# Taking the transposes of q, k and x from the matrix engine to DMA, in a sliding-window attention followed by a dense layer pair

## The chip, the cores and the metric

One core of one Trainium2 chip. The metric is the device time of one execution in microseconds (us). All comparisons are between fast runs. PE is TensorE, ACT ScalarE, DVE VectorE, POOL GpSimd, SP SyncE; on SP nothing but DMA is issued here.

## The reference, cut to what matters

```python
# q, k, v: (8 batches, 8 heads, 576, 64) f32, drawn with 0.1 standard deviation
scores = (1 / sqrt(64)) * q @ k^T
mask   = (0 <= i - j < 64)                 # window of 64, causal
attn   = softmax(where(mask, scores, -1e9))
x      = (attn @ v) as (4608 tokens, 512)  # heads side by side
h      = x @ w_in                          # 512 -> 2048
out    = (h - tanh(h)) @ w_out             # 2048 -> 512
```

## The kernel before

The kernel interleaves two streams of work on PE by hand. One is the pair of dense layers, cut into 9 chunks of 512 tokens with 16 tiles of the hidden layer each; a *half step* is four wide matmuls of the first layer or of the second. The other is the attention, cut into 32 *groups* (a batch and a pair of heads, four groups a batch). `at(h, f)` places a piece of attention behind half step `h`; in the steady part one group takes eight half steps. The first three batches are placed by a script (`PLAN`), batches 3 to 7 by a loop. The matmuls take q, k and x transposed; the kernel transposes them on PE, by matmuls against an identity.

```python
def load_all(b, n):                        # a whole batch of q or k, f32 -> bf16 on the way
    t = all_pool.tile([P, H, E * D], BF16, tag=n, name=n + "all")
    nc.gpsimd.dma_start(out=t, in_=(q if n == "q" else k)[b].rearrange(...))
    # ... (cut)

def keys_v(b, j, eng=nc.sync):             # V's rows into the place of the keys, DMA inside SBUF
    eng.dma_start(out=vw[b % 2][64:128, j]..., in_=vb[8 * j:8 * j + 8]...)

def shift_v(b, j0, j1, eng=nc.sync):       # the same rows once more, shifted by one block of 64
    # ... (cut) one DMA from vw[b % 2][64:128] to vw[b % 2][0:64]

def tr(g, which, bank, *engs):             # six transposes of 96x128 on PE, then copies out of PSUM
    # ... (cut)
    for e in range(E):
        nc.tensor.transpose(tp[:, e, :], src[:, e, :], ident[:P, :P])
    # ... (cut) q: the two heads' halves into separate columns, zeros between; k: as it is

def scores(g, grp, bank):                  # three matmuls of 128 rows x 128 columns, both heads at once
    # ... (cut)
    nc.tensor.matmul(sp[:, i, :], kT[g % NR][:, 64 * j:64 * j + 128],
                     qT[g % NR][:, :, 64 * j:64 * j + 64], ...)
    nc.scalar.activation(PT[...], sp, ACT.Exp, scale=scale)

def y_out(c, s):                           # the second layer's result: copied by ACT, stored by SP
    nc.scalar.activation(ysb, ps[:, yp_bank(c, s), :], ACT.Copy)
    nc.sync.dma_start(out=out[r0:r0 + 128, :], in_=ysb)

for g in range(3 * NP, B * NP):            # batches 3 to 7
    b, pr = divmod(g, NP)
    a = 8 * g - 48
    # ... (cut: casts)
    at(a, tr, g, "q", 3, nc.scalar, nc.vector)
    at(a + 2, tr, g, "k", 3, nc.scalar)
    for i in range(3):
        at(a + 5 + 2 * i, scores, g, i, 4)
    # ... (cut: masking, pv, norm)
    if pr % 2 == 1:
        at(a + 20, x_tr, b, pr // 2, 0, 4, 3)
        at(a + 22, x_tr, b, pr // 2, 4, NJ, 3)
    # ... (cut: keys_v nine times from 32 * b - 54)
    if pr == 0:
        at(32 * b - 78, load_v_all, b)
        at(32 * b - 64, load_all, b, "q")
        at(32 * b - 63, load_all, b, "k")
        at(32 * b - 47, shift_v, b, 0, NJ - 1)
```

The softmax here doesn't subtract the row's maximum and nothing guards it: scores larger than these inputs give would overflow.

## Time and profile before

| kernel before | value | where it is from |
|---|---|---|
| device time, median of 3 | 361.99 us | the runs |
| span of the profiled run | 362.1 us | the page's head |
| PE busy | 326.2 us, 90% | busy by engine |
| PE's mean granted clock | 0.995 | list of cores |
| DMA engines in 120 to 160 us | 0.62 of their time | busy by stretch, last column but one |
| what the chain that ended last consists of | PE 73%, DMA 15% | chain |

The strips, stretches and timelines that this rests on stand in the prediction below. Of the waits of PE, the largest is the first row; each row is "who waits, for whom: us in total, times, longest". The page's row of the hardware DMA queue (packets, megabytes, and the time these packets took as a share of the span of all 16 engines).

```profile
PE ps L197 <- DVE qb L81: 7.7, 2, 6.2
PE ps L224 <- DMA vw<-vw: 0.2, 1, 0.2
```

```profile
q1 hardware_dynamic: 10904, 17.69, 17.0%
```

### The profile page before, as it was taken

How to read it: one execution, taken by the hardware profiler on the slowest of the kernel's cores; microseconds unless marked ns; L12 is line 12 of the kernel's file. 1: busy time of each engine (PE TensorE's matmuls, PEld its weight loads, DVE VectorE, ACT ScalarE, POOL GpSimd, SP SyncE). 2: the span in 40 equal slices, each digit the busy share in tenths (PEclk: the TensorE clock that was granted, in tenths of full speed). 3: DMA queues.
4: the chain of work that ended last, by engine and by line, in shares of the span. 5: the costliest groups of instructions: out<-in, count | busy, mean ns of one | idle time of the engine just before them, and what ended most of it. 6: DMA issues, size and time to landing. Idle time of an engine off the chain costs nothing.

```text
span 362.1 us, 6043 instructions
## 1 busy us (share of the span) xinstructions
PE 326.2 (90%) x2329; PEld 189.5 (52%) x2329; DVE 214.7 (59%) x352; ACT 192.8 (53%) x355; POOL 103.6 (29%) x136
## 2 busy tenths in 40 slices
PE   0538667889999999999999999999999999999995
PEld 0438345655555555555555555555555544444442
DVE  3418657775676776767677767677676633443300
ACT  2536364876656656565656555655564444443421
POOL 7809522806319309312830272110000000000000
PEclk9999998999999999999999999999999999999999
DMA  8899992377876567655935592250000010010012
GB/s 158 128 218 200 216 222 54 54 137 114 202 155 92 97 163 123 129 99 121 139 84 108 128 129 74 58 127 31 30 32 29 31 58 29 31 57 29 31 67 78
DMA packets 31948, 36.76 MB, mean 102 GB/s; under 512 B 3472, under 2 KB 25872, under 8 KB 31536
## 3 DMA queue, kind: packets, MB, share of 16 engines
q0 software_dynamic: 20384, 17.90, 32.7%
q1 hardware_dynamic: 10904, 17.69, 17.0%
q10 hardware_dynamic: 632, 0.79, 0.7%
q8 instruction: 18, 0.29, 0.4%
q14 instruction: 10, 0.08, 0.1%
HBM read 36.70 MB, written 9.44 MB: 127 GB/s over the span
## 4 chain that ended last, share of the span: by engine, by line
PE 73%; DMA 15%; issue 5%; POOL 3%; ACT 2%; DVE 2%; SPq 0%; POOLq 0%; ACTq 0%; DVEq 0%
PE ps L278 32%; PE ps L259 29%; DMA vw<-vb 7%; DMA kall<-in_k_dram 4%; PE ps L224 4%; PE ps L197 3%; PE ps L210 3%; DMA vall<-in_v_dram 2%; PE ps L241 2%; DMA vw<-vw 1%; POOL kb L81 1%; POOL vb L81 1%; DVE qt L81 1%; ACT th L262 1%; POOL qb L81 0%
## 5 line engine op out<-in xcount | busy, mean ns | idle before, releaser
L259 PE MATMUL ps<-xT,wi 128*128 128x512 bf16 x576 | 148.2, 381 | 1.0 <-DVE gT L268 0.9
L278 PE MATMUL ps<-w_out_sb,gT 128*128 128x512 bf16 x576 | 145.2, 379 | 0.2 <-ACT ysb L283 0.2
L268 DVE TENSOR_TENSOR gT<-ps,th 128x512 bf16<-128x512 f32 x144 | 98.9, 690 | 74.2 <-ACT th L262 73.0
L262 ACT ACTIVATE th<-ps 128x512 f32<-128x512 f32 x144 | 86.0, 598 | 85.4 <-PE ps L259 84.1
L259 PEld LDWEIGHTS <-wi 128*128 128x128 bf16 x576 | 61.3, 114 | 47.0 <-issue 2.7
L278 PEld LDWEIGHTS <-gT 128*128 128x128 bf16 x576 | 53.6, 98 | 51.3 <-issue 0.5
L214 ACT ACTIVATE pt<-ps 128x384 bf16<-128x384 f32 x96 | 46.9, 491 | 48.5 <-PE ps L210 37.7
L81 POOL COPY vb<-vall 72x1024 bf16<-72x1024 bf16 x28 | 29.4, 1060 | 71.3 <-DMA vw<-vb 53.9
L235 DVE TENSOR_TENSOR xs<-ps,rc 64x576 bf16<-64x576 f32 x64 | 48.3, 755 | 1.5
L210 PE MATMUL ps<-qt,kt 128*128 128x128 bf16 x288 | 37.3, 230 | 5.6 <-ACT pt L214 3.1
L224 PE MATMUL ps<-vw,pt 128*128 128x130 bf16 x288 | 30.6, 229 | 8.5 <-DVE vw L133 7.1
L224 PEld LDWEIGHTS <-pt 128*128 128x128 bf16 x288 | 22.7, 102 | 22.5 <-issue 7.6
L81 POOL COPY qb<-qall 96x768 bf16<-96x768 bf16 x27 | 22.9, 848 | 36.2 <-PE ps L197 22.9
L81 DVE COPY qt<-ps 64x576 bf16<-64x576 bf16 x33 | 25.0, 757 | 12.9 <-ACT qt L79 8.3
L81 POOL COPY kb<-kall 96x768 bf16<-96x768 bf16 x28 | 23.6, 847 | 28.9 <-DMA kall<-in_k_dram 11.1
L210 PEld LDWEIGHTS <-kt 128*128 128x128 bf16 x288 | 25.0, 104 | 10.8 <-ACT kt L79 2.4
L283 ACT ACTIVATE ysb<-ps 128x512 f32<-128x512 f32 x36 | 21.4, 594 | 15.1 <-PE ps L278 15.1
L81 DVE COPY xT<-ps 128x512 bf16<-128x512 bf16 (+4 forms) x35 | 12.1, 368 | 16.8 <-PE ps L241 16.8
L197 PE MATMUL ps<-ident,qb 96*128 96x96 bf16 x192 | 14.4, 215 | 7.9 <-DVE qb L81 7.7
L79 ACT ACTIVATE qt<-ps 64x576 bf16<-64x576 bf16 x31 | 19.7, 635 | 3.5 <-PE ps L197 1.9
L79 ACT ACTIVATE kt<-ps 128x576 bf16<-128x576 bf16 x30 | 19.4, 645 | 2.6 <-PE ps L197 1.5
L197 PE MATMUL ps<-ident,kb 96*128 96x96 bf16 x192 | 14.4, 214 | 5.7 <-ACT kb L79 4.6
(47 smaller groups left out, 148.0 us busy)
## 6 DMA issues: line engine op xcount, KB each, us to landing
out_dram<-ysb SPq DMA_DIRECT2D x36, 256.0 KB
vw<-vb SPq DMA_DIRECT2D x67, 65.0 KB
vall<-in_v_dram POOLq DMA_DIRECT2D x7, 576.0 KB, 9.2
kall<-in_k_dram POOLq DMA_DIRECT2D x7, 576.0 KB, 10.2
qall<-in_q_dram POOLq DMA_DIRECT2D x7, 576.0 KB, 6.3
vw<-vw SPq DMA_DIRECT2D x6, 520.0 KB
w_out_sb<-in_moe_w_out_dram POOLq DMA_DIRECT2D x4, 512.0 KB, 13.3
wi<-in_moe_w_in_dram POOLq DMA_DIRECT2D x2, 512.0 KB, 14.0
```

What stands on the lines that cost most here:

```text
L79: nc.scalar.activation(o, i, ACT.Copy)
L81: eng.tensor_copy(o, i)
L197: nc.tensor.transpose(tp[:, e, :], src[:, e, :], ident[:P, :P])
L210: nc.tensor.matmul(sp[:, i, :], kT[g % NR][:, 64 * j:64 * j + 128], qT[g % NR][:, :, 64 * j:64 * j + 64], start=True, stop=g >= 2 * NP)
L214: nc.scalar.activation(PT[g % NPT][:, 3 * grp:3 * grp + 3, :], sp, ACT.Exp, scale=scale)
L224: nc.tensor.matmul(ps[:, 5 + grp, 130 * i:130 * i + 130], PT[g % NPT][:, j, :], vw[b % 2][:, j, 2 * pr:2 * pr + 2, :], start=True, stop=True)
L235: nc.vector.tensor_tensor(xo[r, :, :, pr, :], ov[r, :, :, h, 0:D], rc[r].to_broadcast([64, 3, 3, 64]), ALU.mult)
L259: nc.tensor.matmul(hp, w_in_tile(ki, m), chunk_tile(c)[:, ki, :], start=(ki == 0), stop=(ki == 3))
L262: nc.scalar.activation(th, hp, ACT.Tanh)
L268: nc.vector.tensor_tensor(gT[c][:, m, :], hp, th, ALU.subtract)
L278: nc.tensor.matmul(yp, gT[c][:, m, s * 128:(s + 1) * 128], w_out_sb[:, m, :], start=(m == 0), stop=(m == M - 1))
L283: nc.scalar.activation(ysb, ps[:, yp_bank(c, s), :], ACT.Copy)
```

## The change

The intent: take work off PE, the bound engine. In batches 3 to 7, q and k (already bf16) go through a scratch tensor in DRAM and come back transposed by DMA, two groups at a time; the output x of the attention is transposed by DMA straight into the dense layer's input. With q no longer padded with zeros, a score block is two matmuls of 64 rows, one for each head, on the upper and the lower half of the PE array ("row tiles"). The loads of q and k are issued ten half steps earlier, and the script of the first three batches was rewritten.

```diff
+    def bounce(n):                                  # SBUF -> DRAM
+        t = dram.tile([S, 256], BF16, tag=n, name=n + "d")
+        nc.sync.dma_start(out=t.rearrange("(p e) c -> p (e c)", e=E),
+                          in_=two[n].rearrange("p e i h d -> p (e i h d)"))
+        two[n] = t
+    def tr2(g, n):                                  # DRAM -> SBUF, transposed
+        o = qT2[g // 2 % 2] if n == "q" else kT2[g // 2 % 2][:, :, 64:]
+        nc.sync.dma_start(out=o, in_=two.pop(n), transpose=True)
+    def x_dma(b):                                   # two or three pieces, one for each chunk touched
+        ...
+            nc.sync.dma_start(out=chunk_tile(c)[...], in_=xs[b % 2][...], transpose=True)
+    def scores2(g, grp):
+        ...
+        for w in range(3):
+            j = 3 * grp + w
+            for h in range(2):
+                r = slice(64 * h, 64 * h + 64)
+                nc.tensor.matmul(sp[:, w, h, :], kT2[i][r, g % 2, 64 * j:64 * j + 128],
+                                 qT2[i][r, g % 2, 64 * j:64 * j + 64], start=True, stop=True)
 ... (cut: the new script of batches 0 to 2, buffers, the layout of xT)
     for g in range(3 * NP, B * NP):
-        a = 8 * g - 48
-        at(a, tr, g, "q", 3, nc.scalar, nc.vector)
-        at(a + 2, tr, g, "k", 3, nc.scalar)
+        a = 8 * g - 50
+        if pr % 2 == 0:
+            for i, n in enumerate("qk"):
+                at(a - 15 + 2 * i, cast2, g, n)
+                at(a - 14 + 2 * i, cast2, g + 1, n)
+                at(a - 12 + 2 * i, bounce, n)
+                at(a - 7 + 2 * i, tr2, g, n)
-            at(a + 5 + 2 * i, scores, g, i, 4)
+            at(a + 5 + 2 * i, scores2, g, i)
-        if pr % 2 == 1:
-            at(a + 20, x_tr, b, pr // 2, 0, 4, 3)
-            at(a + 22, x_tr, b, pr // 2, 4, NJ, 3)
+        if pr == NP - 1:
+            at(a + 18, x_dma, b)
-            at(32 * b - 64, load_all, b, "q")
-            at(32 * b - 63, load_all, b, "k")
+            at(32 * b - 74, load_all, b, "q")
+            at(32 * b - 73, load_all, b, "k")
```

## The prediction

Its sum came to -4.4 us, so 357.6, and the forecast to 358.5. Three terms are in part estimate:

- Mode switches (+8.4): the 0.07 us a switch was chosen between the extra of 0.107 us behind the mask's transpose, the one such place in the trace before, and half of that, since the clock had doubled by then. What PE does in that time is not shown.
- Row tiles (-2.0): that two of them can run at once was not shown before the change ran; the 28 ns a matmul and so the 5 us are worked out from the trace, the 0.4 is a guess. That weight loads lie hidden, which speaks for it, is read from the line for 120 to 160 us: PEld was busy for 23.35 of the 40 us (its second busy time) in which PE was busy for 40.00.
- Transfers (+1.5): from the 3.1 us for x's first piece and the two loads the author went on to about 8 us, the lead that x has, with a doubling for sharing and a latency that are not shown. "The trace has them" speaks of the DMA engines: their share is 0.62 and 0.57 in the lines for 120 to 200 us.

> **What bounds the kernel now.** I first read the busy shares in 40 slices, to see which stages there are, then the busy time by stretch.
>
> ```profile
> PE   0538667889999999999999999999999999999995
> ACT  2536364876656656565656555655564444443421
> DMA  8899992377876567655935592250000010010012
> ...
> 120.00:160.00 40.00, 40.00 (x301) 23.35 (x300) 27.93 (x48) 23.56 (x45) 15.99 (x19) 1.00 0.62 117
> 160.00:200.00 40.00, 40.00 (x304) 23.46 (x303) 28.98 (x47) 24.50 (x47) 12.72 (x15) 1.00 0.57 112
> 280.00:320.00 40.00, 40.00 (x198) 20.01 (x197) 17.70 (x29) 17.27 (x29) 0.00 (x0) 1.00 0.11 40
> ```
>
> There are three stages. Up to about 90 us PE has gaps and the DMA engines are full. From 90 to about 277 us the dense layers and the attention of the later batches share a full PE. After that the dense layers run alone. DVE (28 of 40 us) and ACT (24 of 40) bound neither later stage, so copies taken from them are worth nothing by themselves. The chain that ended last says the same: PE holds 73% of it.
>
> ```profile
> PE 73%; DMA 15%; issue 5%; POOL 3%; ACT 2%; DVE 2%; SPq 0%; POOLq 0%; ACTq 0%; DVEq 0%
> ```
>
> A busy PE is not a PE at its peak, so I read start times in the timeline of PE.
>
> ```profile
> 158.97 0.33 PE L210 MATMUL ps<-qt,kt 128*128 128x128 bf16 x3
> 159.14 1.03 PE L259 MATMUL ps<-xT,wi 128*128 128x512 bf16 x4
> 160.00 0.42 PE L197 MATMUL ps<-ident,qb 96*128 96x96 bf16 x6
> 160.37 1.02 PE L278 MATMUL ps<-w_out_sb,gT 128*128 128x512 bf16 x4
> 161.23 0.33 PE L210 MATMUL ps<-qt,kt 128*128 128x128 bf16 x3
> 161.40 1.03 PE L259 MATMUL ps<-xT,wi 128*128 128x512 bf16 x4
> 162.26 0.42 PE L197 MATMUL ps<-ident,kb 96*128 96x96 bf16 x6
> 162.52 0.38 PE L278 MATMUL ps<-w_out_sb,gT 128*128 128x512 bf16 x1
> ```
>
> From start to start four wide matmuls take 0.86 us (0.215 each), three score matmuls 0.17 us (0.056 each), and six k transposes 0.26 us (0.042 each). But the six q transposes take 0.37: 0.11 of it is a wait. The timeline of ACT at the same place names it.
>
> ```profile
> 159.34 0.49 ACT L214 ACTIVATE pt<-ps 128x384 bf16<-128x384 f32 x1 [0.72 <-PE ps L210]
> 159.73 0.59 ACT L283 ACTIVATE ysb<-ps 128x512 f32<-128x512 f32 x1
> ```
>
> The exp of the scores stands ahead of the output copy on ACT; the copy ends at 160.32, and only then may the second dense layer write its bank again (160.37). Once per eight half steps this happens. Where no q transpose stands in that place, the wait is seen whole:
>
> ```profile
> 273.68 1.03 PE L259 MATMUL ps<-xT,wi 128*128 128x512 bf16 x4
> 274.91 1.02 PE L278 MATMUL ps<-w_out_sb,gT 128*128 128x512 bf16 x4 [0.20 <-ACT ysb L283]
> ```
>
> 1.23 us from the start of the first layer's four matmuls to the second's, 0.86 of work and 0.37 of wait. So the q transposes lie wholly in the shadow of this wait, the k transposes do not.
>
> [...] The kernel before holds one instruction with 64 active rows, the transpose of the mask:
>
> ```profile
> 17.98 0.23 PE L183 MATMUL ps<-ident,seen 64*128 64x64 bf16 x1
> 18.14 0.42 PE L197 MATMUL ps<-ident,kb 96*128 96x96 bf16 x3
> ```
>
> 0.16 us pass to the next start. There the clock is still at half (128-column matmuls start 0.107 apart), so the 64 columns should take 0.053. About 0.107 is extra, with no wait recorded[...]. [...] No transpose by DMA is in the trace before, so no run shows it yet. [...] The trace has them 0.5 to 0.6 busy in the middle stage, so new traffic will queue with old.
>
> **The change part by part.** It touches 20 groups (head pairs) of 32, those of batches 3 to 7. The built program has 150 fewer matmuls.
>
> - Removed on PE: 12 transposes in each of 20 groups, 240 x 0.0417 = 10.0 us. Nine x transposes twice a batch for five batches, 90 x 0.057 = 5.1 us. Together 15.1 us.
> - The wait for the output copy stays, since score group 3 of the new schedule still stands just ahead of it, and nothing now fills it. It grows from 0.11 to 0.37 us less one switch of mode (0.07, below) that delays PE beside it: 0.30. Over 20 groups +3.8 us.
> - Scores: nine matmuls of 128 columns (9 x 0.056 = 0.50 us a group) become 18 of 64 columns. By the slope between 96 and 512 columns (0.418 ns a column and 1.5 ns) one takes 28 ns, so 18 take 0.51: no change if the two row tiles follow one another. If they run at once, 0.25 to 0.3 us a group is saved, 5 us in all. Each needs its own weight load of 128 columns, which may forbid it. I give it 0.4, so -2.0.
> - Mode switches: the scores of a group come in three places, each between 128-row matmuls, so six switches a group, 120 in all. Per switch I take [...]0.07. 120 x 0.07 = +8.4 us. This is the choice on which the sum hangs.
> - Copies: ACT loses 1.28 us and DVE 0.76 us a group plus the x copies. Off the path: 0. POOL makes as many copies as before.
> - Transfers: a pair of groups writes and rereads q and k through DRAM (each 295 KB), x moves 590 KB a batch. That is 5.9 + 5.9 + 2.95 = 14.7 MB more. The hardware queue's 17.69 MB took 17.0% of the span, 3.5 us a MB over 16 engines, so an estimate of 51 us of all engines over some 130 us: their share goes from about 0.55 to 0.9. The q and k transposes are issued 12 and 10 half steps (10 us or more) before use, which covers it. x is issued only eight half steps (about 8 us) before the first layer reads it, behind a q transpose and an output store on the same queue, while the next loads of q and k are issued. At 3.5 us a MB, x's first piece and those two (0.88 MB) take 3.1 us[...]. I expect little or no wait, at most 1 to 3 us at the first three chunks: +1.5.
> - Early stage: the script of the first three batches was rewritten. PE waited about 16 us between 40 and 120 us, so there is room, but also room to lose. Its loads of the first dense weights are issued later, those of the second batch's q earlier. I take -1 with 2.5 either way.
>
> Sum: -15.1 + 3.8 - 2.0 + 8.4 + 1.5 - 1.0 = -4.4, so about 357.6. Transfers can only add, so my median is 358.5.
>
> **The rivals.** (a) *The transposes come off PE almost freely*: switches cost 0.03 us or less, row tiles overlap. Then -15.1 + 4 - 5 + 3.6 - 1, about 348 us. For it: weight loads lie hidden everywhere in the trace before. Against it: the 0.16 us after the mask. (b) *Switches cost 0.12 us or more*: 14 us and no overlap give about +2, 364 us. For it: that 0.107 may be a fixed time, and entering the mode may cost more than leaving it. (c) *Transfers become the bound*: [...]x and then q and k come late, PE stands at each chunk, and 5 to 30 us are lost, 365 to 390. For it: the engines are already half busy and x has the smallest lead. Against it: the leads of q and k are ten half steps, and x's first piece shrinks from chunk to chunk. (d) *The early stage decides*: +-3 us whatever the middle does.
>
> **Range and chances.** Switches (+-3), overlap (-5 or 0) and the early stage (+-2.5) give about +-5 around 358; rival (c), at 0.15, stretches the upper side. Range 351 to 368. Faster by over 2% means under 354.8: it needs overlap or cheap switches, 0.30. Slower by over 2% means over 369.2: it needs (c) or dear switches with a bad early stage, 0.15 to 0.2. Within 2%: 0.5.
>
> **What would show each step.** In the timeline of PE of the changed kernel: score matmuls 28 ns apart (14 if tiles overlap); from the last matmul before a score group to the first of it, and on leaving, about 0.07 us more than the matmul's own time; 1.23 us from the first layer to the second at every eighth half step. Groups of 128x64 score matmuls: 360. PE's idle time by releaser should show no large entry from DMA to the first dense layer at 128 to 250 us; if it shows several us there, (c) was right. The first dense matmul should start near 40 us as now. I am wrong in the main if the middle stage's time per group changes by more than 0.4 us either way from 8.8 us (my sum: 8.8 - 0.76 + 0.19 - 0.1 + 0.42 = 8.55).

## The result, and the profile after

The changed kernel took 383.53 us (median of 4 fast runs, 382.12 to 384.88), the kernel before 361.86 us in the same rounds (4 runs, 361.65 to 362.25). The ratio is 1.060, with a 95% interval of 1.056 to 1.064: slower. Ratios in this document are the mean time of one kernel's fast runs over that of the other's of the same rounds, so not quite the ratio of the medians that are quoted. The prediction was 358.5 us with a range of 351 to 368; it was wrong.

First the strips of the changed kernel (40 slices of 9.5 us, busy tenths; PEclk is the granted clock), its stretches, and its chain by engine.

```profile
PE   1466879869849995989699979899999999999995
PEclk9999899998997998999899999999999999999999
DMA  8999995976994599779979897957700131001012
...
PE 52%; DMA 35%; ACT 4%; issue 3%; POOL 2%; DVE 1%; SPq 1%; POOLq 0%; DVEq 0%; ACTq 0%
```

```profile
120.00:160.00 40.00, 35.26 (x238) 17.64 (x241) 20.14 (x33) 17.99 (x34) 10.63 (x14) 0.96 0.75 149
160.00:200.00 40.00, 34.99 (x232) 17.26 (x235) 19.98 (x32) 17.00 (x33) 12.83 (x17) 0.96 0.90 175
280.00:320.00 40.00, 39.57 (x220) 19.80 (x224) 20.61 (x32) 18.14 (x32) 0.00 (x0) 1.00 0.16 48
```

PE, which was busy for 40.00 of 40 us in the two middle stretches, now has holes of five us in each, and its clock falls below full around them. The DMA share rose from 0.57 to 0.90 in the second one. In the chain PE gave up 21 points and DMA gained 20. (The third stretch now holds the last of the attention, since everything is later. 31 records of the second layer's matmuls are missing from this trace, so PE's busy time is slightly too low; the starts used below don't depend on them.) The waits of PE name the transfers:

```profile
PE ps L251 <- DMA kt<-kd: 9.4, 3, 3.8
PE ps L274 <- DMA vw<-vw: 7.8, 3, 4.0
...
PE ps L307 <- DMA xT<-xs: 2.9, 3, 1.5
```

20 us of waits for DMA in three rows, where the kernel before had 0.2. The second row, V's shift inside SBUF, is a transfer that the change doesn't touch.

**Where the time went, by half step.** Since both kernels run the same 288 half steps of dense work, the start of the same first-layer tile in both traces can be subtracted. The table gives "this kernel minus before" in us, from the traces; the last columns are experiments told below.

| half step | after | script only | k behind q | no q/k transfers | x only | x only, loads early |
|---|---|---|---|---|---|---|
| 0 | -2.30 | -1.45 | -0.80 | -1.84 | -2.09 | -1.76 |
| 40 | -5.72 | -4.25 | -4.42 | -5.33 | -5.63 | -5.37 |
| 64 | +6.52 | -3.97 | +8.65 | +7.59 | -5.36 | -5.09 |
| 80 | +6.16 | -3.97 | +8.29 | +7.23 | -5.86 | -5.60 |
| 88 | +11.35 | -3.97 | +8.36 | +7.30 | -5.86 | -5.60 |
| 96 | +12.09 | -3.97 | +11.24 | +6.87 | -3.47 | -6.10 |
| 112 | +11.49 | -3.97 | +12.19 | +6.52 | -2.53 | -6.60 |
| 120 | +16.58 | -3.97 | +12.26 | +6.59 | -2.53 | -6.60 |
| 144 | +15.93 | -3.96 | +13.14 | +5.80 | -2.98 | -7.61 |
| 160 | +20.43 | -3.96 | +15.17 | +5.45 | -2.44 | -8.11 |
| 224 | +18.36 | -3.94 | +14.78 | +3.62 | -4.50 | -10.12 |

The column "after" adds up from four kinds of pieces. Up to half step 40 the kernel gains 5.7 us, of which the script alone gave 4.2 in run 1. Two waits for V cost 12.2 between 40 and 64. Five more steps upward (k at 80 to 88: 5.2; 0.7 for x; k at 112 to 120: 5.1; k at 144 to 152: 2.5; V and x at 152 to 160: 2.0) cost 15.5. In the undisturbed stretches between them the kernel gains 3.7 in all. -5.7 + 12.2 + 15.5 - 3.7 = 18.3, the difference of the two spans.

**How one k comes late.** Here are PE's wait in the timeline of PE, the chain's piece across it, the timeline of SP, and the timeline of POOL (all of the changed kernel; columns: start, us, engine, operation; the bracket is idle time and its releaser).

```profile
147.00 0.34 PE L251 MATMUL ps<-qt,kt 64*128 64x64 bf16 x6 [3.77 <-DMA kt<-kd]
147.27 1.90 PE L307 MATMUL ps<-xT,wi 128*128 128x512 bf16 x4
```

```profile
131.06 0.60 ACT ysb L332
...
132.13 14.82 DMA kt<-kd
```

```profile
126.87 1.29 SPq L231 DMA_TRANSPOSE qt<-qd  x1
131.67 0.35 SPq L334 DMA_DIRECT2D out_dram<-ysb  x1
132.13 4.33 SPq L231 DMA_TRANSPOSE kt<-kd  x1
```

```profile
130.81 0.77 POOL L103 DMA_DIRECT2D qall<-in_q_dram  x1
131.57 0.78 POOL L103 DMA_DIRECT2D kall<-in_k_dram  x1
```

q's transpose is issued at 126.87. The next thing on SP is the store of an output tile, and that waits for ACT's copy, which ends at 131.66. k's transpose stands behind it and goes out at 132.13, five us after q's, although it had been ready before (run 2 below issues it 1.34 us after q's). By then POOL has issued the next batch's loads of V, q and k (129.99, 130.81 and 131.57). The transfer takes 14.82 us from issue to landing; the records of its packets lie between 137.6 and 144.9 us, so for over five us it moved nothing. Ten half steps of lead in the program became no lead at all.

What it stood behind can be seen on the output stores, which go out on the same queue. Their first packet moves 0.83 to 1.3 us after the issue at most places of this trace, but 4.1 to 4.7 us after it at four places (98.2, 131.7, 172.2 and 211.8 us), each 0.1 to 3.9 us behind POOL's issue of a load of k. The trace before has the same delay, 2.6 to 4.2 us at five places, so it could have been read before predicting.

The wait costs more than its own length. Behind it four wide matmuls take 1.90 us instead of 1.05: their starts are 0.427 us apart instead of 0.216. In this trace, from half step 40 on, the four waits of 3.04 to 4.04 us are followed by half clock, those of 2.35 us and less are not; in run 9 it follows a wait of 2.72 us. Half clock is recorded for 3.41 or 6.83 us at a time; the part of it behind the wait cost 1.4 to 2.6 us each time (an estimate: half of that part).

**The middle stage itself** answers to the lines that the prediction showed of one score place:

```profile
134.29 0.33 PE L274 MATMUL ps<-vw,pt 128*128 128x130 bf16 x3
134.55 0.26 PE L251 MATMUL ps<-qt,kt 64*128 64x64 bf16 x6
134.75 1.05 PE L307 MATMUL ps<-xT,wi 128*128 128x512 bf16 x4
```

From the raw starts: the last of the three matmuls at L274 starts at 134.400, the first score at 134.553, the last score at 134.623, the next wide matmul at 134.746. The two tiles of a pair start 3 ns apart, so I read them as running at once, and pairs start 29 to 38 ns apart. But 0.153 us pass on the way in, of which 0.056 is the matmul's own, and 0.123 on the way out, of which 0.028 is (an estimate: the prediction's slope between 96 and 512 columns): 0.097 and 0.095 us of extra, and 0.026 more at the next start (0.242 instead of 0.216). So the place takes 0.290 us (134.400 to 134.746 less 0.056 of the last matmul before it) and 0.026, 0.316 in all. Three full score matmuls took 0.167. Three places a group make that 0.45 us more.

### The profile page after: what moved, and what is told of

It reads as the page before. It is cut to its first block, busy times and chain, and to the rows that moved or that the text cites. A ratio compares the mean times of both kernels' runs of the same rounds, so it can differ in the third digit from the quotient of the medians.

```text
span 380.4 us, 5640 instructions
## 1 busy us (share of the span) xinstructions
PE 324.8 (85%) x2148; PEld 172.7 (45%) x2179; DVE 189.5 (50%) x304; ACT 173.6 (46%) x316; POOL 103.9 (27%) x138
## 3 DMA queue, kind: packets, MB, share of 16 engines
q1 hardware_dynamic: 48520, 32.30, 34.5%
## 4 chain that ended last, share of the span: by engine, by line
PE 52%; DMA 35%; ACT 4%; issue 3%; POOL 2%; DVE 1%; SPq 1%; POOLq 0%; DVEq 0%; ACTq 0%
PE ps L327 24%; PE ps L307 21%; DMA vw<-vb 15%; DMA kt<-kd 11%; DMA vw<-vw 5%; PE ps L274 3%; DMA xT<-xs 3%; ACT ysb L332 2%; PE ps L251 2%; DMA vall<-in_v_dram 1%; POOL vb L86 1%; ACT th L311 1%; PE ps L260 1%; POOL vall L117 1%; DVE vw L138 1%
## 5 line engine op out<-in xcount | busy, mean ns | idle before, releaser
L307 PE MATMUL ps<-xT,wi 128*128 128x512 bf16 x576 | 153.3, 391 | 4.4 <-DMA xT<-xs 2.9
L274 PE MATMUL ps<-vw,pt 128*128 128x130 bf16 x288 | 31.8, 233 | 13.4 <-DMA vw<-vw 7.8
L274 PEld LDWEIGHTS <-pt 128*128 128x128 bf16 x288 | 23.6, 104 | 30.8 <-DMA vw<-vw 8.4
L220 POOL COPY qb<-qall 96x768 bf16<-96x768 bf16 x20 | 16.0, 826 | 39.0 <-DMA qd<-qb 37.3
L260 PE MATMUL ps<-qt,kt 128*128 128x128 bf16 x108 | 16.9, 241 | 8.4 <-ACT pt L264 7.4
L251 PE MATMUL ps<-qt,kt 64*128 64x64 bf16 x360 | 15.8, 195 | 9.7 <-DMA kt<-kd 9.4
L251 PEld LDWEIGHTS <-kt 64*128 64x128 bf16 x360 | 8.7, 95 | 23.4 <-issue 10.0
L268 DVE TENSOR_TENSOR pt<-pt,ps 128x1152 bf16<-128x1152 bf16 x24 | 17.9, 744 | 1.7 <-ACT pt L264 1.7
L220 POOL COPY kb<-kall 96x768 bf16<-96x768 bf16 x20 | 16.0, 827 | 3.2 <-DMA kall<-in_k_dram 3.2
L260 PEld LDWEIGHTS <-kt 128*128 128x128 bf16 x108 | 11.2, 110 | 5.1 <-issue 2.2
L263 PE MATMUL ps<-hide,ident 128*128 128x128 bf16 x72 | 13.1, 254 | 0.0
L281 DVE RECIPROCAL rc<-ps 128x9 f32<-128x9 f32 x32 | 6.8, 213 | 12.3 <-PE ps L274 12.2
## 6 DMA issues: line engine op xcount, KB each, us to landing
kall<-in_k_dram POOLq DMA_DIRECT2D x7, 576.0 KB, 17.2
qall<-in_q_dram POOLq DMA_DIRECT2D x7, 576.0 KB, 14.6
```

The costliest lines, as they stand in the source:

```text
L220: nc.gpsimd.tensor_copy(two[n][:, :, i].rearrange("p e h d -> p h e d"), stage.pop((g, n)).rearrange("p h (e d) -> p h e d", d=D))
L251: nc.tensor.matmul(sp[:, w, h, :], kT2[i][r, g % 2, 64 * j:64 * j + 128], qT2[i][r, g % 2, 64 * j:64 * j + 64], start=True, stop=True)
L274: nc.tensor.matmul(ps[:, 5 + grp, 130 * i:130 * i + 130], PT[g % NPT][:, j, :], vw[b % 2][:, j, 2 * pr:2 * pr + 2, :], start=True, stop=True)
L307: nc.tensor.matmul(hp, w_in_tile(ki, m), chunk_tile(c)[:, :, ki % 2, 64 * (ki // 2):64 * (ki // 2) + 64], start=(ki == 0), stop=(ki == 3))
```

## The experiments

The columns of the table above are runs 1, 2, 3, 9 and 11. All kernels passed the comparison with the reference. "Run 1" to "run 12" number the experiments. They ran on three chips, so ratios are compared. The expectations of runs 10 and 11 came true; that of run 7 did in part; in the others the first-named outcome was missed, or (run 4) could not be told from its rival.

### 1. The new script alone

Edit: the kernel before with the changed kernel's `PLAN` and nothing else.

> The kernel before with only the rewritten script for the first three batches. In the changed kernel the half step 32 is reached 5.4 us earlier than before. If that gain comes from the script alone, this run takes 356 to 358 us and reaches half step 32 near 71 us. If it needs something else of the change (other pools, x in another layout, earlier loads), it stays at 360 to 364.

Measured: 359.51 us (358.47 to 360.70), before 363.51, ratio 0.989 (0.984 to 0.995). By half step it gains its 4 us before half step 32 (reached at 72.7 us, not 71), and after 64 its curve moves by 0.03 us. So the script is no cause of the loss: it is worth 4 us, and what the changed kernel lost elsewhere is that much more.

### 2. k's transpose straight behind q's

```diff
-                at(a - 7 + 2 * i, tr2, g, n)
+                at(a - 7, tr2, g, n)
```

> The changed kernel, k transpose issued straight after the q transpose, ahead of the output store that the SP queue waits for. Theory 1 (late issue: k stands behind a store that waits for ACT, and so falls into the next batch's loads): the three waits of TensorE for k of 3.9, 3.4 and 2.5 us vanish with the half-clock time after them, 12 to 15 us less, 369 to 372 us; the k transposes of a batch's first pair land within 5 us of issue. Rival (the DMA engines are simply full, so order does not matter): the wait moves to another transfer and the time stays within 4 us of 383.5.

Measured: 376.29 us (375.41 to 378.53), ratio 1.036 (1.031 to 1.042). The timeline of SP shows the edit doing what it should, k being issued ahead of the output store:

```profile
128.79 1.29 SPq L231 DMA_TRANSPOSE qt<-qd  x1
130.13 1.43 SPq L231 DMA_TRANSPOSE kt<-kd  x1
133.81 0.35 SPq L334 DMA_DIRECT2D out_dram<-ysb  x1
```

All waits for k are gone from PE's list. In their place, of this run:

```profile
PE ps L274 <- DMA vw<-vw: 8.3, 2, 5.2
PE ps L307 <- DMA xT<-xs: 7.2, 3, 3.0
```

The gain is 7 us by the medians and 8 by the ratios, where removing the k waits and nothing else would have given 12 to 15 by the expectation. So the order on SP is a cause, and the rival (the engines are full, and a transfer that goes first makes another late) is right about a part of the rest: x, now behind k, waits 7.2 us instead of 2.9.

### 3. No q and k transfers from the second loop batch on (wrong on purpose)

```diff
-                at(a - 12 + 2 * i, bounce, n)
-                at(a - 7 + 2 * i, tr2, g, n)
+                if g < 16:
+                    at(a - 12 + 2 * i, bounce, n)
+                    at(a - 7 + 2 * i, tr2, g, n)
```

> Wrong on purpose: from the fifth batch on the stores and transposes of q and k are left out (old data is used), all else stays. If the transfers cost all that was lost, TensorE has no wait for k any more and little for x and V after the fourth batch: 361.9 - 5.4 (early stage) - 3.6 (0.18 us in each of 20 groups) + about 8 (waits for V up to half step 64, which stay) = 360 to 364 us. If the row tiles and mode switches were the cost, it stays near 380.

Measured: 367.47 us (366.46 to 368.23), ratio 1.011 (1.005 to 1.017). The scores of batches 4 to 7 use old q and k. It still passed the comparison with the reference: with inputs of 0.1 the scores are so small that the softmax is nearly even over the window. So that comparison does not guard q and k here; a reader who edits these parts must check them otherwise.

From half step 64 on PE is idle for less than 0.1 us per eight half steps, and the curve falls from +7.59 to +3.62. That is what the middle stage gives when nothing comes late: 4 us over 20 groups. Expected were 360 to 364 us; the miss is the two V waits between 40 and 64, 12.9 us here, which stayed since batch 3 kept its transfers.

### 4. Row tiles in turn instead of alternating

```diff
-        for w in range(3):
-            j = 3 * grp + w
-            for h in range(2):
+        for h in range(2):
+            for w in range(3):
```

> The changed kernel with the six score matmuls of a place ordered by head: three on the lower row tile, then three on the upper. If the two row tiles really run at once in the changed kernel (starts 3 ns apart, pairs 28 ns apart), this order must lose it or keep only part: starts 28 ns apart, up to 0.08 us more at each of 60 places, up to 5 us more where TensorE bounds, 384 to 388 us. If the start times in the trace are only recorded so, nothing changes (within 1 us of 383.5).

Measured: 384.16 us (382.26 to 385.68), ratio 1.057 (1.051 to 1.063): the same as the changed kernel. In the trace a score place looks the same too:

```profile
255.46 0.27 PE L251 MATMUL ps<-qt,kt 64*128 64x64 bf16 x6
255.66 1.06 PE L307 MATMUL ps<-xT,wi 128*128 128x512 bf16 x4
```

In another such place the six records start at 251.257, .267, .296, .305, .325 and .334: still in pairs, 29 to 39 ns from pair to pair, although the three of the lower half were issued first. The records don't name the half, but two matmuls of one half, at 28 ns each by the same estimate, would hardly start 10 ns apart; I read it as overlap of the halves across the order of issue, which is not shown. Either way the order is not where the loss is.

### 5. The loads of q and k later

```diff
-            at(32 * b - 74, load_all, b, "q")
-            at(32 * b - 73, load_all, b, "k")
+            at(32 * b - (74 if b == 3 else 66), load_all, b, "q")
+            at(32 * b - (73 if b == 3 else 66), load_all, b, "k")
```

> The changed kernel with the loads of q and k of the batches 4 to 7 put behind the first two casts of that batch's V on GpSimd, so that they can no longer run beside the V copies and the first k transpose of the batch before. Theory (loads that come too early fill the DMA engines just when V copies and the k transpose are due): the 4 to 5 us wait for V of the fourth batch (half step 59) falls to under 2 us, the three waits for k go, 383.5 becomes 362 to 370 us. Rival (the engines are full whatever the order): q and k of the next batch come late instead and the time stays over 376.

Measured: 388.19 us (382.54 to 388.93), ratio of the fast runs 1.060 (1.049 to 1.072). Two of its four runs, the profiled one among them, were over 1.5% above the fastest and so count as slow; its profile is not used here. From the times alone: moving the loads away from k's transposes gained nothing. The next run keeps this edit, in a profile of a fast run.

### 6. Loads later, and the order on SP mended

On top of run 5: k straight behind q for the first pair of a batch, and x two half steps earlier, ahead of the second pair's q and k.

```diff
-                at(a - 7 + 2 * i, tr2, g, n)
+                at(a - 7 + (0 if pr == 0 else 2 + i), tr2, g, n)
-            at(a + 18, x_dma, b)
+            at(a + 16, x_dma, b)
```

> As the run before, with the first pair's k transpose straight behind its q transpose, and x's transposes two half steps earlier and ahead of the second pair's. If issue order matters beside the loads, the waits for x (1.3 and 0.5 us) go too: 358 to 366 us, and 1 to 4 us below the run before. If only the loads mattered, equal to it within 1 us.

Measured: 373.75 us (372.16 to 374.99), ratio 1.028 (1.023 to 1.034). Expected were 358 to 366. It is the best of the versions that keep the whole change, and still with waits of 6.8 us for x, 4.8 for V's shift and 3.3 for k in PE's list. Each re-spacing took one wait away and left or lengthened others.

### 7. Only the earlier loads, on top of the script

```diff
 (the kernel of run 1)
-            at(32 * b - 64, load_all, b, "q")
-            at(32 * b - 63, load_all, b, "k")
+            at(32 * b - 74, load_all, b, "q")
+            at(32 * b - 73, load_all, b, "k")
```

> The kernel before with the new script for the first batches and the q and k loads ten half steps earlier, as the changed kernel has them, but no transpose by DMA at all. In the run without q and k transposes the waits for V between half steps 40 and 64 still cost 12 us. If the early loads alone cause them, they show here: half steps 40 to 64 take 4 to 12 us longer than in the kernel with the new script alone (30.2 us), 363 to 371 us. If the extra transfers are needed for it, the time stays at 358 to 360.

Measured: 362.75 us (360.98 to 364.61), ratio 0.998 (0.992 to 1.004). Beside run 1's ratio the earlier loads cost about 3 us, without any transpose by DMA. By half step all of it comes between 40 and 48, where PE waits 3.1 us for V's shift; from 64 on it is flat. In the changed kernel the first V wait stands in the same place and the second (half steps 56 to 64) comes on top. So one of the two V waits is the loads' doing, and the second needs the new transfers of batch 3 as well. It needs the early loads of batch 4 too: with these eight half steps later, it is 1.5 us in run 6 and gone in run 8, where it was 4.0 in the changed kernel. But then k is late for 3.3 and 3.9 us at half step 66, so most of the loss stays.

### 8. q and k by DMA, x on PE

The loads late and k first as in run 6, and `x_tr` back in place of `x_dma`.

> The changed kernel with late loads and k straight after q, and x transposed on TensorE again as before. TensorE gets 90 transposes back (5.1 us), the DMA engines lose 2.95 MB. If x by DMA is free once nothing is late, this is 3 to 6 us slower than the run with x by DMA. If DMA is the bound, it is equal or faster.

Measured: 371.92 us (370.39 to 373.30), ratio 1.023 (1.018 to 1.029; whether it is slower by 2% is unclear). Two things follow. With x back on PE and 90 transposes more it is no slower than run 6 (the intervals touch), so x by DMA did not pay beside q and k. And after half step 96, where no transfer is late any more, it moves from +5.53 to +6.48 against the kernel before: +0.06 us a group. So q and k by DMA with scores as row tiles saves *nothing*, even when every transfer is in time.

### 9. x by DMA alone

Script and `x_dma` (at `a + 16`) kept; q, k, scores and loads as in the kernel before.

> Only two parts of the change: the new script for the first batches and x transposed by DMA; q and k stay on TensorE, loads as before. The script alone gave 3.9 us. The 90 x transposes are 5.1 us of TensorE time, and the runs say that x by DMA costs only where k and q transposes and early loads stand in its way. So 361.9 - 3.9 - 5 = 352 to 355 us, faster than both kernels. If x by DMA is late by itself, waits of over 1 us show at the starts of chunks 3 to 7 and it is 357 to 365.

Measured: 359.25 us (356.05 to 365.00, 6 runs, the longest slow), ratio 0.989 (0.985 to 0.993). Where nothing is late it gains 0.25 us a group, what the removed x transposes are worth. But x comes late at three chunks (2.72, 0.46 and 0.89 us); the first of them in the timeline of PE:

```profile
147.12 1.90 PE L303 MATMUL ps<-xT,wi 128*128 128x512 bf16 x4 [2.72 <-DMA xT<-xs]
```

The transfers' records say why. x's transpose is issued at 137.6, behind an output store of 136.9. POOL's loads of q and k were issued at 135.1 and 136.7, and neither the store nor the transpose moves a packet until 140.6. From 143 to 145 the transpose and the load of k move as many packets as each other, 184 to 187 a us each; but the transpose's have 256 bytes and the load's 768, and they take 0.36 and 0.9 of the engines' time. The loads end at about 145.5, and it is through two us later. The line also shows the clock halved (1.90 for four) after 2.72 us of idle.

### 10. Full-width scores on old data (wrong on purpose)

Run 3, with the scores of batches 4 to 7 as nine full matmuls in place of the row tiles.

```diff
-            at(a + 5 + 2 * i, scores2, g, i)
+            at(a + 5 + 2 * i, *((scores2, g, i) if g < 16 else (scores, g, i, 4)))
```

> Wrong on purpose: the run without q and k transposes, its scores from the fifth batch on computed as before (nine matmuls of 128 columns over all rows, on old data). Nothing else differs. By the start times in the trace a place of six row-tile matmuls costs TensorE 0.32 us with both switches of mode, three full matmuls 0.17: 0.45 us a group, 16 groups, less about 0.1 us a group that the wait for the output copy takes up: 5 to 7.5 us less than that run (367.5), 360 to 362. If switches are free and overlap counts, it is 3 us slower.

Measured: 361.71 us (360.26 to 363.04), ratio 0.998 (0.994 to 1.001), against run 3's 1.011. From half step 72 to 224 it gains 9.3 us where run 3 gains 4.0: the row tiles with their switches of mode cost 0.33 us a group (5.3 over 16 groups), after the wait for the output copy is netted. This is the run that separates them from the transfers. Here that wait is seen whole again, as in the prediction (0.37 from start to start), whereas a switch in its shadow had cut it to 0.247.

### 11. x by DMA, with the loads of q and k out of its way

```diff
 (the kernel of run 9)
-            at(32 * b - 64, load_all, b, "q")
-            at(32 * b - 63, load_all, b, "k")
+            at(32 * b - (64 if b == 3 else 74), load_all, b, "q")
+            at(32 * b - (63 if b == 3 else 73), load_all, b, "k")
```

> The kernel with the new script and x by DMA, its q and k loads of the batches 4 to 7 ten half steps earlier. In the run before, TensorE waited 2.9 and 1.1 us for x at chunks 3 and 5, and in the DMA records x's transposes moved only after the loads of q and k that started just ahead of them. If it is the loads, both waits fall under 0.3 us and the profile shows 352 to 354 us instead of 357.6 (ratio to before 0.97 to 0.98), with no wait for V over 1 us after half step 64. If x waits anyway, 357 to 360.

Measured: **353.58 us** (352.49 to 356.09, 6 fast runs), before 362.92 (11 runs), ratio 0.975 (0.972 to 0.978). Faster than both kernels. Its stretches and its chain by engine:

```profile
120.00:160.00 40.00, 40.00 (x291) 22.84 (x289) 27.55 (x42) 24.97 (x48) 12.64 (x15) 1.00 0.83 154
160.00:200.00 40.00, 40.00 (x295) 23.03 (x294) 27.38 (x43) 25.28 (x49) 12.63 (x15) 1.00 0.69 140
...
PE 81%; ACT 6%; DMA 6%; DVE 3%; POOL 2%; issue 1%; SPq 0%; ACTq 0%; POOLq 0%; DVEq 0%
```

PE is busy throughout at full clock, although the DMA share is 0.83 in the first stretch: it isn't the share by itself that makes PE wait. Run 9 had a lower share there (0.75) and waited; the two differ only in when q and k are loaded, so it is what stands in front of the transfer that is needed next. The curve falls by 5.0 us from half step 64 to 224, the whole worth of 90 x transposes.

### 12. Run 11 with the scores one half step earlier

```diff
-            at(a + 5 + 2 * i, scores, g, i, 4)
+            at(a + 4 + 2 * i, scores, g, i, 4)
```

> As the run before, with each group's score matmuls half a step earlier, so that ACT copies the dense output ahead of the exp and not behind it. If the wait of 0.11 us once per group (0.25 in the changed kernel) is due to that order on ACT, it goes: 1.5 to 2.5 us less than the run before. If not, equal within 0.5 us.

Measured: 358.66 us (357.40 to 360.90, 6 runs), ratio 0.989 (0.986 to 0.992): worse than run 11. The 0.11 us wait for the output copy is gone, but now the exp stands ahead of ACT's copy of q, DVE's copy of the other half follows that, and the transposes of k wait for their bank, 18 times up to 0.4 us. A try to gain the last tenth gave back five us.

```profile
160.25 0.42 PE L200 MATMUL ps<-ident,kb 96*128 96x96 bf16 x6 [0.23 <-DVE qt L84]
```

## Why the prediction was wrong

- **Transfers, "+1.5": the step that failed.** Measured in its place: two of the four kinds of pieces above give 12.2 + 15.5 = 27.7 us. This is PE's 20 us of waits for DMA plus some seven us at half clock behind them (an estimate: 1.7, 2.6, 1.4 and 1.7 us for the four stretches). The 1.5 us was meant for x, and of the 20 us x has only 2.9, near the 1 to 3 expected; k (9.4) and V (7.8) had been given no wait at all. The prediction named an outcome of this size, rival (c), and gave it 0.15, but (c) put x first and laid it to slow transposes. What made the step fail:
  1. *Lead was counted in half steps of the program, not from the issue on SP.* "12 and 10 half steps (10 us or more) before use, which covers it" overlooked that an output store, which waits for ACT, stood between q and k on SP: in the lines above k goes out at 132.13, behind the store of 131.67, and 5 us of lead are gone. Run 2 shows that this was worth 7 to 8 us, and that mending it alone moved part of the wait to x.
  2. *Transfers that the change doesn't touch were not looked at.* V's copy and shift are issued on SP like the new transfers, just ahead of their use; 12.2 us are theirs. Runs 7 and 3 show them in the kernel with earlier loads alone (one wait) and with batch 3's transfers (both). The diff shows the loads of q and k moved by ten half steps; the prediction does not price this.
  3. *The transfers were sized too small.* It took 3.5 us of all engines for a megabyte, 51 us in all. The page's row of the queue now reads:

```profile
q1 hardware_dynamic: 48520, 32.30, 34.5%
```

  34.5% of 380.4 us less 17.0% of 362.1 us is 69.7 us for 14.6 MB more, 4.8 us a MB. The records split it: 34,560 transposing packets of 256 bytes at 23.1 ns each on average, 49.9 us of 16 engines for 8.85 MB (5.6 us a MB, or 177 GB/s), others running beside them included, and 1,920 packets of the stores to scratch at 143.5 ns, 17.2 us. Where no other packets moved (128 to 129.5 us), some 860 transposing packets a us went through, 220 GB/s. Size alone is not the cause, though: run 11 is at a share of 0.83 in one stretch without a wait.
  4. *A wait was priced at its length.* Half clock behind it makes one of 3.77 us cost 5.2 (half steps 80 to 88 of the table).
- **Early stage, "-1 with 2.5 either way":** right in sign, but the gain was larger than that range allows. Run 1 gives 4 us; within the changed kernel it was 5.7 at half step 40. This hid part of the loss.
- **Mode switches, "120 x 0.07 = +8.4":** 0.097 going in and 0.095 + 0.026 coming out were measured, 0.218 for the two, so 13.1 us over 60 places. Rival (b) was right that it is nearly a fixed time: the one place that lies wholly at half clock (114.2 us) took 0.141 in and 0.101 out, the next start included, 0.24 for the two, and not double. The hedge in the middle was the wrong choice.
- **Row tiles, "0.4, so -2.0":** by their starts, 3 ns apart, they ran at once, 0.21 us a group saved in the stream of scores, 4.2 us. With the switches the scores cost 0.45 us a group more than before by the timeline, and 0.33 net of the output copy's wait by run 10; the prediction had 0.32 before that wait.
- **The wait for the output copy, "0.30":** 0.247, so +2.7 us instead of +3.8. Nearly right.
- **Middle stage, 8.55 us a group:** 8.61 between the waits. The sum was -15.1 + 3.8 - 2.0 + 8.4 = -4.9 us, against the -3.7 measured. That it came so close is in part luck: the switches were 4.7 us too cheap, and the row tiles and the wait for the output copy 2.2 and 1.1 too dear. And it is the part that moved the time by 4 us; the part that moved it by 28 was put at 1.5.
- **The expected gain**, 15 us of transposes off PE, thus went two ways. The ten us of q and k were lost in place, to mode switches and to a wait that q's transposes had filled (run 8: +0.06 us a group). Run 10 shows the first half of this: with full-row scores the changed kernel gains 0.49 us a group from half step 72 to 224, so 0.24 more than x's 0.25 (on old data, without the transfers). The five us of x are real (run 11), but with q's and k's transfers beside it they could not be had.

What stays open: why SP's queue moves nothing for about four us behind POOL's loads of q and k (the traces show it, nothing here explains it); and whether q and k by DMA with full-row scores, q's zeros kept, would pay with the transfers in time. No run tried that. Run 5 by itself can't be read, its profile being of a slow run.

## What to carry to other kernels

Before work is moved from a full engine to DMA, list for each new transfer what is ahead of it on its issuing queue, including stores that wait for an engine, and what other queues start at that time; count the lead from there in us, and look at the old transfers that the new ones will make late. Take the part of such a change that saves the bound engine something in place (x here, 0.25 us a group) and leave the part whose saving is eaten on the same engine (q and k here, by mode switches and a wait that nothing fills any more). When one wait is mended, look at once at the list of waits for the next: in run 2, with the DMA engines at 0.83 and 0.95 of their time between 120 and 200 us, the waits for k went and those for x rose from 2.9 to 7.2 us.
